# Q, K and V by one level of Strassen, with left-hand sums shared by the three products and with five-bank product chains

## The chip, the cores and the metric

The kernel runs on one core of a Trainium2 chip. The metric is the device time of one execution in microseconds (us). "Work of TensorE" below means matmuls counted in the trace, times the spacing that a steady stream of them shows in the same trace: 0.216 us for one with 512 columns, 0.06 us for one with 132. What a stage takes beyond its work is called "lost".

## The reference

```python
# x: 2048 x 1024, H = 32 heads of 32, F = 3584, all bf16
q, k, v = split(layernorm(x) @ wqkv)             # 3 products 2048x1024x1024
phi = lambda t: where(t > 0, t + 1, exp(t)) + 1e-6
kv  = einsum("bhsd,bhse->bhde", phi(k), v)       # needs every token
z   = einsum("bhsd->bhd", phi(k))
o   = (phi(q) @ kv) / (phi(q) @ z + 1e-6)
h   = x + o @ wo
hn  = layernorm(h)
out = h + (relu(hn @ W_gate) * (hn @ W_up)) @ W_down
```

## The kernel before

TensorE goes through five stages: a start-up; K, V and the sums kv over all 16 token tiles; Q, attention and four early blocks of the MLP, woven into each other; 24 wide MLP blocks; the down projection. MLP and down projection are computed by one level of Strassen already (7 products of half size instead of 8). Q, K and V are plain.

```python
abpool = tile_pool(name="abpool", bufs=2, space=PSUM)    # vp, attn
pspool = tile_pool(name="ps", bufs=3, space=PSUM)        # tp, kp, qp
ndpool = tile_pool(name="ndpool", bufs=3, space=PSUM)    # nd, in the attention stage
...
def kproj(t):                                  # one tile of 128 tokens
    for j in range(2):
        ps = bank("kp")
        for kc in range(KC):                   # 8 matmuls of 128x512
            nc.tensor.matmul(ps[:], lhsT=xnT[:, kc, t * P:(t + 1) * P],
                             rhs=wkv_sb[:, kc, j * NW:(j + 1) * NW], ...)
        phi_from_psum(ps[:], pk[:, j * NW:(j + 1) * NW], NW)
...
AHEAD = 2
for t in range(AHEAD): ln_T(t)                 # LayerNorm and transpose
for g in range(ST // NT):                      # 4 groups of 4 tiles
    for t in group(g):
        if t + AHEAD < ST: ln_T(t + AHEAD)     # stands before the first kproj
        pks[t] = kproj(t)
    for t in group(g): vproj_kv(t, pks.pop(t))
for c in range(KC): q_proj(qblocks[0], c)
...
LAG = (0, 1, 2, 3)             # a tile: nd, oT, output projection, transpose of hn
STS = ST // NS                 # 8 tiles in a half of the tokens
QSTEPS = 3 * ST // NS // 2     # 12 steps with Q in them
for step in range(QSTEPS):
    attn_step(step)            # tile n runs its stage k in step n + LAG[k]
    for b, c in rest[...]: q_proj(b, c)
psctx.close()
early = [load_group(g) for g in range(NE // GP)]   # weights of the early MLP blocks
for n, step in enumerate(range(QSTEPS, ST + 3)):
    attn_step(step)
    for p in flow[...]: p()    # parts of the early MLP blocks
```

When the last tile of a half has gone through `hn_T`, four VectorE additions of 128x2048 build the Strassen sums of that half; the first MLP blocks need those of the first half. All DMA of the kernel is issued from one queue, that of SyncE.

Of the kernel before, what the change touches and what calls it, by code (L numbers as in the profile page):

```python
# [8 lines left out]
ALU = mybir.AluOpType  # L9
# [22 lines left out]
def block_kernel(ctx: ExitStack, tc: tile.TileContext, x, wqkv, wo, wg, wu, wd, out, H: int):  # L32
# [41 lines left out]

    abctx = ExitStack()
    abpool = abctx.enter_context(tc.tile_pool(name="abpool", bufs=2, space=PSUM, side="right"))
    psctx = ExitStack()
    pspool = psctx.enter_context(tc.tile_pool(name="ps", bufs=3, space=PSUM))

    def bank(nm, dt=FP32, shape=None):  # L80
        return pspool.tile(shape or [P, NW], dt, tag="b", name=nm)
# [4 lines left out]
    pqT = pq_pool.tile([P, KC, S], BF16, name="pqT")  # L86
    kvz = pq_pool.tile([P, KC, NDW], BF16, name="kvz")
    wo_sb = pq_pool.tile([P, KC, D], BF16, name="wo_sb")
# [4 lines left out]
    qwork = qctx.enter_context(tc.tile_pool(name="qwork", bufs=2, side="right"))  # L93
    wq_sb = qpool.tile([P, KC, D], BF16, name="wq_sb")
    xnT = qpool.tile([P, KC, S], BF16, name="xnT")
    wqkv_v = wqkv.rearrange("(kc p) n -> p kc n", p=P)

    def phi_from_psum(ps_ap, dst_ap, width):
        e = qwork.tile([P, width], FP32, tag="phi_e", name="phi_e")
        nc.scalar.activation(out=e[:], in_=ps_ap, func=ACT.Exp)  # L100
        e2 = qwork.tile([P, width], FP32, tag="phi_e2", name="phi_e2")
        nc.vector.tensor_scalar(out=e2[:], in0=e[:], scalar1=1.0, scalar2=PHI_EPS,
                                op0=ALU.min, op1=ALU.add)
        nc.vector.scalar_tensor_tensor(out=dst_ap, in0=ps_ap, scalar=0.0, in1=e2[:],  # L104
                                       op0=ALU.max, op1=ALU.add)

    def q_proj(b, c):
        ps = bank("qp")
        for kc in range(KC):
            nc.tensor.matmul(ps[:], lhsT=wq_sb[:, kc, c * P:(c + 1) * P],  # L110
                             rhs=xnT[:, kc, b * SW:(b + 1) * SW], start=(kc == 0), stop=(kc == KC - 1))
        phi_from_psum(ps[:], pqT[:, c, b * SW:(b + 1) * SW], SW)

    def layernorm(src, stats, dst, small):

        mv = small.tile([P, nc.vector.BN_AGGR_DIM], FP32, tag="mv", name="mv")
        nc.vector.bn_aggr(out=mv[:], in_=stats[:])
        lnv = small.tile([P, 1], FP32, tag="lnv", name="lnv")
        nc.scalar.activation(out=lnv[:], in_=mv[:, 1:2], func=ACT.Ln, bias=LN_EPS, scale=1.0)
        rstd = small.tile([P, 1], FP32, tag="rstd", name="rstd")  # L120
        nc.scalar.activation(out=rstd[:], in_=lnv[:], func=ACT.Exp, scale=-0.5)
        nc.vector.tensor_scalar(out=dst[:], in0=src[:], scalar1=mv[:, 0:1], scalar2=rstd[:],
                                op0=ALU.subtract, op1=ALU.mult)
# [3 lines left out]
    qblocks = [order[k] // NT for k in range(0, ST, NT)]  # L127
# [3 lines left out]
    n_kv = (KC + GPB - 1) // GPB  # L131
    with ExitStack() as actx:
        apool = actx.enter_context(tc.tile_pool(name="apool", bufs=1))
        xpool = actx.enter_context(tc.tile_pool(name="xpool", bufs=6))
        awork = actx.enter_context(tc.tile_pool(name="awork", bufs=2))
        asmall = actx.enter_context(tc.tile_pool(name="asmall", bufs=4))
        wkv_sb = apool.tile([P, KC, 2 * D], BF16, name="wkv_sb")
        kvpool = actx.enter_context(tc.tile_pool(name="kvpool", bufs=n_kv, space=PSUM))
# [3 lines left out]
        def load_x(t):  # L142
            x_sb = xpool.tile([P, D], BF16, tag="x_sb", name="x_sb")
            nc.sync.dma_start(out=x_sb[:], in_=xf[t * P:(t + 1) * P, :])
            x_tiles[t] = x_sb
# [4 lines left out]
        load_x(0)  # L150
        load_w(wkv_sb, 0, D)
        load_x(1)
        load_w(wkv_sb, 1, D)
        load_x(2)
        load_x(3)
        load_w(wkv_sb, 2, D)
        load_w(wkv_sb, 3, D)
        load_x(4)
        load_x(5)
        for j in range(2):  # L160
            load_w(wq_sb, j, 0)
        nc.sync.dma_start(out=wo_sb[:], in_=wo.rearrange("(kc p) n -> p kc n", p=P))

        def ln_T(t):
            if t not in x_tiles:
                load_x(t)
            x_sb = x_tiles.pop(t)
            stats = asmall.tile([P, 2, nc.vector.BN_STATS_DIM], FP32, tag="stats", name="stats")
            for i in range(2):
                nc.vector.bn_stats(out=stats[:, i, :], in_=x_sb[:, i * NW:(i + 1) * NW])  # L170
            xn = awork.tile([P, D], BF16, tag="xn", name="xn")
            layernorm(x_sb, stats, xn, asmall)
            if t >= PE_T:
                nc.sync.dma_start_transpose(out=xnT[:, :, t * P:(t + 1) * P], in_=xn[:])
                return
            for i in range(2):
                pt = bank("tp", BF16, [P, KH, P])
                for kc in range(KH):
                    nc.tensor.transpose(pt[:, kc, :], xn[:, (i * KH + kc) * P:(i * KH + kc + 1) * P], ident[:])
                (nc.scalar.copy if i else nc.vector.tensor_copy)(  # L180
                    out=xnT[:, i * KH:(i + 1) * KH, t * P:(t + 1) * P], in_=pt[:])

        def kproj(t):
            pk = awork.tile([P, D], BF16, tag="pk", bufs=NT + 2, name="pk")
            for j in range(2):
                ps = bank("kp")
                for kc in range(KC):
                    nc.tensor.matmul(ps[:], lhsT=xnT[:, kc, t * P:(t + 1) * P],  # L188
                                     rhs=wkv_sb[:, kc, j * NW:(j + 1) * NW],
                                     start=(kc == 0), stop=(kc == KC - 1))  # L190
                phi_from_psum(ps[:], pk[:, j * NW:(j + 1) * NW], NW)
            return pk

        def vproj_kv(t, pk):
            v_sb = awork.tile([P, KC, NDW], BF16, tag="v_sb", name="v_sb")
            nc.gpsimd.memset(v_sb[:, :, P:NDW], 1.0)
            for j in range(2):
                ps = abpool.tile([P, NW], FP32, tag="ab", name="vp")
                for kc in range(KC):
                    nc.tensor.matmul(ps[:], lhsT=xnT[:, kc, t * P:(t + 1) * P],  # L200
                                     rhs=wkv_sb[:, kc, D + j * NW:D + (j + 1) * NW],
                                     start=(kc == 0), stop=(kc == KC - 1))
                nc.scalar.copy(out=v_sb[:, j * KH:(j + 1) * KH, 0:P],  # L203
                               in_=ps[:].rearrange("p (c e) -> p c e", e=P))
            for c in range(KC):
                bnk, i = divmod(c, GPB)
                nc.tensor.matmul(kv_ps[bnk][:, i * NDW:(i + 1) * NDW],
                                 lhsT=pk[:, c * P:(c + 1) * P], rhs=v_sb[:, c, :],
                                 start=(t == 0 and i == 0), stop=(t == ST - 1),
                                 skip_group_check=True)  # L210

        PE_T = 4
        AHEAD = 2
        for t in range(AHEAD):
            ln_T(t)
        for g in range(ST // NT):
            pks = {}
            for t in range(g * NT, (g + 1) * NT):
                if t + AHEAD < ST:
                    ln_T(t + AHEAD)  # L220
                pks[t] = kproj(t)
            for t in range(g * NT, (g + 1) * NT):
                vproj_kv(t, pks.pop(t))
# [4 lines left out]
        for c in range(KC):  # L228
            q_proj(qblocks[0], c)
# [3 lines left out]
    ndpool = psctx.enter_context(tc.tile_pool(name="ndpool", bufs=3, space=PSUM))  # L233
    aops = mctx.enter_context(tc.tile_pool(name="aops", bufs=1))

    hnT = [[aops.tile([P, KC, SW], BF16, name=f"hn{s}{i}") for i in range(2)] for s in range(NS)]
    hns = [[aops.tile([P, KH, SW], FP16, name=f"hs{s}{k}") for k in range(3)] for s in range(NS)]
    pieces = [(c, min(GPB, KC - c)) for c in range(0, KC, GPB)]

    def strassen_sums(out, a11, a12, a21, a22, eng):  # L240

        s1, s2, s3, s4 = out
        eng.tensor_tensor(out=s1, in0=a21, in1=a22, op=ALU.add)
        eng.tensor_tensor(out=s2, in0=s1, in1=a11, op=ALU.subtract)
        eng.tensor_tensor(out=s3, in0=a11, in1=a21, op=ALU.subtract)
        eng.tensor_tensor(out=s4, in0=a12, in1=s2, op=ALU.subtract)

    def hn_blocks(s):
        return [[hnT[s][i][:, j * KH:(j + 1) * KH, :] for j in range(2)] for i in range(2)]

    def attn_stages(t, late):
# [5 lines left out]
        def nd():  # L257
# [3 lines left out]
            for c0, n in pieces:  # L261
                ps = (abpool if late else ndpool).tile([P, NW], FP32, tag="ab" if late else "nd", name="nd")
# [12 lines left out]
        def oT():  # L275
            st["oT"] = bwork.tile([P, KC, P], BF16, tag="oT", name="oT")
            nc.sync.dma_start_transpose(out=st["oT"][:], in_=st["o"][:])
            x_sb = bwork.tile([P, D], BF16, tag="x_res", bufs=3, name="x_res")
# [372 lines left out]
```

## Time and profile before

788.15 us median of the first three runs (788.11 to 789.91). The head of the profile's page gives the span and each engine's busy time:

```profile
span 786.4 us, 9532 instructions
...
PE 755.9 (96%) x3602; PEld 347.9 (44%) x3664; DVE 459.1 (58%) x848; ACT 261.5 (33%) x457; POOL 3.6 (0%) x32
```

TensorE (PE) is 96% busy: it bounds the kernel. How its time falls into stages is read from its timeline (where the first matmul of each kind starts); the table of windows then gives the busy time of every engine in them. The rows are K/V, Q with attention and early MLP, the wide MLP blocks, and the down projection; the columns are length, busy time (with the number of instructions) of each engine, granted clock, DMA share and GB/s.

```profile
core 0: us, PE busy (x) PEld busy (x) DVE busy (x) ACT busy (x) POOL busy (x), PEclk, DMA share, GB/s
15.16:141.21 126.05, 123.03 (x640) 58.64 (x652) 57.54 (x118) 42.33 (x90) 2.00 (x14) 1.00 0.37 95
141.21:312.47 171.26, 165.51 (x835) 77.41 (x847) 124.71 (x347) 86.95 (x184) 0.00 (x0) 0.99 0.57 130
312.47:612.97 300.50, 295.40 (x1336) 132.83 (x1360) 169.83 (x280) 127.70 (x172) 0.00 (x0) 1.00 0.24 70
612.97:786.40 173.43, 169.06 (x775) 76.61 (x784) 98.98 (x89) 0.58 (x1) 0.00 (x0) 1.00 0.51 171
```

The first two rows hold the stages that the change touches.

```profile
312.47 1.03 PE L386 MATMUL A<-hn_1499,wg 128*128 128x512 bf16 x3
316.13 1.02 PE L386 MATMUL E<-hs_1503,wg 128*128 128x512 f16 x4 [0.29 <-DVE gu L405]
```

There is little waiting to remove. What can be removed is matmuls, and the start: TensorE's timeline (start, length, engine, line, operation, count, in brackets the idle time before it and what ended it) shows three tiles' transposes ahead of the first K matmul.

```profile
6.26 1.04 PE L179 MATMUL tp<-ident,xn 128*128 128x128 bf16 x8 [6.26 <-DVE xn L122]
10.22 1.04 PE L179 MATMUL tp<-ident,xn 128*128 128x128 bf16 x8 [2.92 <-DVE xn L122]
14.34 1.03 PE L179 MATMUL tp<-ident,xn 128*128 128x128 bf16 x8 [3.08 <-DVE xn L122]
15.16 5.09 PE L188 MATMUL kp<-wkv_sb,xnT 128*128 128x512 bf16 x13
```

The list of TensorE's waits (us in all, times, longest) has besides these only small entries:

```profile
PE tp L179 <- DVE xn L122: 12.3, 3, 6.3
PE nd L264 <- DVE o_sb L271: 2.2, 1, 2.2
PE A L386 <- ACT snap L400: 2.0, 2, 1.1
```

### The profile page before, as it was taken

The numbers are of one execution on the slowest core, as the hardware profiler recorded it, in microseconds if no ns is written. First come the engines' busy times: TensorE is split into PE (matmuls) and PEld (weight loads), VectorE is DVE, ScalarE is ACT, GpSimd is POOL, SyncE is SP. The second block draws the span as 40 slices with busy tenths as digits, with TensorE's granted clock in tenths as the row PEclk, the third lists the DMA queues.
The fourth block names the chain that finished last, engine by engine and source line by source line (L and its number), as shares of the span: only waits on it lengthen the run. The fifth ranks groups of instructions, "written<-read, shape, count | busy, mean of one in ns | idle before, by whom it ended". The sixth has DMA issues, their size and how long they took to land.

```text
span 786.4 us, 9532 instructions
## 1 busy us (share of the span) xinstructions
PE 755.9 (96%) x3602; PEld 347.9 (44%) x3664; DVE 459.1 (58%) x848; ACT 261.5 (33%) x457; POOL 3.6 (0%) x32
## 2 busy tenths in 40 slices
PE   3989999999998999999999999999999999999998
PEld 2444444444443444444444444444444444444443
DVE  4783412576688667757456464564644992439722
ACT  2333323346555545444434444444444000000000
POOL 0000000000000000000000000000000000000000
PEclk9999999999999999999999999999999999999999
DMA  9991000045659834453204032140100896881001
GB/s 319 308 188 27 1 1 1 1 93 133 151 111 263 194 101 120 155 140 92 64 33 128 8 99 55 35 127 8 46 5 31 271 285 206 299 307 50 27 28 53
DMA packets 125150, 89.76 MB, mean 114 GB/s; under 512 B 50352, under 2 KB 116912, under 8 KB 124592
## 3 DMA queue, kind: packets, MB, share of 16 engines
q1 hardware_dynamic: 125104, 89.15, 40.2%
q8 instruction: 28, 0.46, 0.3%
q14 instruction: 18, 0.15, 0.1%
HBM read 59.77 MB, written 17.83 MB: 99 GB/s over the span
## 4 chain that ended last, share of the span: by engine, by line
PE 63%; DVE 16%; ACT 6%; issue 4%; DMA 3%; SPq 0%; DVEq 0%; ACTq 0%
PE A L386 17%; PE accA L521 10%; PE E L386 9%; PE accE L521 6%; PE vp L200 5%; DVE gu L405 4%; PE kp L188 4%; PE qp L110 3%; PE Dp L386 3%; PE attn L288 3%; ACT snap L400 2%; PE accD L521 2%; ACT hn L300 1%; DVE x_res L290 1%; ACT gu L407 1%
## 5 line engine op out<-in xcount | busy, mean ns | idle before, releaser
L405 DVE TENSOR_TENSOR gu<-E,snap 128x1024 bf16<-128x1024 f32 x56 | 68.4, 1222 | 98.5 <-ACT snap L400 95.9
L400 ACT COPY snap<-A 128x1024 f32<-128x1024 f32 x84 | 84.0, 1007 | 92.3 <-PE A L386 92.2
L407 ACT ACTIVATE gu<-gu 128x512 bf16<-128x512 bf16 x84 | 52.9, 630 | 100.9 <-DVE gu L405 100.5
L521 PEld LDWEIGHTS <-hh 128*128 128x128 bf16 (+1 forms) x560 | 54.7, 98 | 67.7 <-issue 1.9
L521 PE MATMUL accA<-wd,hh 128*128 128x512 f16 (+1 forms) x333 | 73.2, 379 | 1.6 <-DVE gu L405 1.4
L386 PEld LDWEIGHTS <-tg 128*128 128x128 f16 x448 | 43.7, 98 | 59.3 <-issue 9.2
L386 PEld LDWEIGHTS <-tu 128*128 128x128 f16 x448 | 43.8, 98 | 52.6
L288 PE MATMUL attn<-wo_sb,oT 128*128 128x512 bf16 x250 | 60.0, 386 | 1.0 <-DVE rd L270 0.7
L188 PE MATMUL kp<-wkv_sb,xnT 128*128 128x512 bf16 x250 | 58.3, 389 | 1.2 <-DVE pk L104 0.8
L200 PE MATMUL vp<-wkv_sb,xnT 128*128 128x512 bf16 x249 | 59.2, 379 | 0.3
L110 PE MATMUL qp<-xnT,wq_sb 128*128 128x512 bf16 x250 | 57.0, 379 | 0.2
L386 PEld LDWEIGHTS <-wu 128*128 128x128 bf16 x336 | 32.9, 98 | 39.6
L386 PEld LDWEIGHTS <-wg 128*128 128x128 bf16 x336 | 32.7, 98 | 39.9 <-issue 1.6
L188 PEld LDWEIGHTS <-xnT 128*128 128x128 bf16 x256 | 25.3, 100 | 31.3 <-issue 4.1
L405 DVE TENSOR_TENSOR gu<-Dp,snap 128x1024 bf16<-128x1024 f32 x28 | 34.1, 1220 | 6.3 <-ACT snap L400 4.4
L110 PEld LDWEIGHTS <-wq_sb 128*128 128x128 bf16 x256 | 24.9, 98 | 29.0
L288 PEld LDWEIGHTS <-oT 128*128 128x128 bf16 x256 | 24.6, 99 | 29.0 <-issue 3.8
L200 PEld LDWEIGHTS <-xnT 128*128 128x128 bf16 x256 | 24.0, 98 | 24.3
L203 ACT CAST v_sb<-vp 128x512 bf16<-128x512 f32 x32 | 18.7, 584 | 39.0 <-PE vp L200 39.0
L386 PE MATMUL A<-hn_1500,tg 128*128 128x512 f16 (+1 forms) x111 | 28.7, 379 | 1.2 <-ACT snap L400 1.1
L300 ACT ACTIVATE hn<-x_res,sm 128x1024 bf16<-128x1024 bf16 x16 | 18.3, 1146 | 34.2 <-DVE sm L299 29.4
L386 PE MATMUL A<-hn_1498,tg 128*128 128x512 f16 (+1 forms) x112 | 28.7, 379 | 0.9 <-ACT snap L400 0.9
(359 smaller groups left out, 1016.2 us busy)
## 6 DMA issues: line engine op xcount, KB each, us to landing
wd<-in_B_W_down_dram SPq DMA_DIRECT2D x16, 896.0 KB, 6.5
wg<-in_B_W_gate_dram SPq DMA_DIRECT2D x14, 512.0 KB, 5.1
wu<-in_B_W_up_dram SPq DMA_DIRECT2D x14, 512.0 KB, 5.0
x_sb<-in_A_x_dram SPq DMA_DIRECT2D x16, 256.0 KB, 4.0
wkv_sb<-in_A_wqkv_dram SPq DMA_DIRECT2D x4, 1024.0 KB, 9.3
x_res<-in_A_x_dram SPq DMA_DIRECT2D x16, 256.0 KB, 3.1
out_dram<-o SPq DMA_DIRECT2D x32, 128.0 KB, 2.1
wq_sb<-in_A_wqkv_dram SPq DMA_DIRECT2D x2, 1024.0 KB, 11.0
```

Of the source, the lines that this page charges most:

```text
L110: nc.tensor.matmul(ps[:], lhsT=wq_sb[:, kc, c * P:(c + 1) * P], rhs=xnT[:, kc, b * SW:(b + 1) * SW], start=(kc == 0), stop=(kc == KC - 1))
L188: nc.tensor.matmul(ps[:], lhsT=xnT[:, kc, t * P:(t + 1) * P], rhs=wkv_sb[:, kc, j * NW:(j + 1) * NW], start=(kc == 0), stop=(kc == KC - 1))
L200: nc.tensor.matmul(ps[:], lhsT=xnT[:, kc, t * P:(t + 1) * P], rhs=wkv_sb[:, kc, D + j * NW:D + (j + 1) * NW], start=(kc == 0), stop=(kc == ...
L203: nc.scalar.copy(out=v_sb[:, j * KH:(j + 1) * KH, 0:P], in_=ps[:].rearrange("p (c e) -> p c e", e=P))
L288: nc.tensor.matmul(ps[:], lhsT=st["oT"][:, c, :], rhs=wo_sb[:, c, j * NW:(j + 1) * NW], start=(c == 0), stop=(c == KC - 1))
L290: nc.vector.scalar_tensor_tensor(out=h_sb[:, j * NW:(j + 1) * NW], in0=ps[:], scalar=1.0, in1=h_sb[:, j * NW:(j + 1) * NW], op0=ALU.mult, ...
L300: nc.scalar.activation(out=st["hn"][:], in_=h_sb[:], func=ACT.Square, bias=nmean, scale=1.0, accum_out=var)
L386: nc.tensor.matmul(ps[:, v, :], lhsT=w[v][m - 1][:, kc, :], rhs=left[m - 1][:, kc, :], start=(start and kc == 0), stop=(kc == KH - 1), ski ...
L400: nc.scalar.copy(out=m[:], in_=ps[:])
L405: nc.vector.tensor_tensor(out=gu[:], in0=ps[:], in1=m[:], op=ALU.add)
L407: nc.scalar.activation(out=gu[:, 0, :], in_=gu[:, 0, :], func=ACT.Relu)
L521: nc.tensor.matmul(accs[tt][:], lhsT=lhs[:, half * FD + f, tt * P:(tt + 1) * P], rhs=rhs[half][:, f, :], start=(start and half == 0 and f ...
```

## The change

It aims at TensorE's work. One Strassen unit covers four token tiles (K, V) or four 128-column strips of Q's output, with 56 matmuls instead of 64. K and V stay plain for the first four tiles, so that the kernel can start before any sums exist. Q's 256 matmuls become 224, the 512 of K and V become 464: 80 fewer, 17.3 us at 0.216 us each. The left-hand sums of the normalized x are made once and serve Q, K and V.

The products of a unit go through five PSUM banks (tags A and E with two each, D with one), and partial results are copied out by ScalarE ("snapshots"). The same chain, called `narrow`, now serves the four early MLP blocks. That leaves attention two `ab` banks and a single `nd` bank. Buffers are shared: K's weights lie where Q's result comes later, pk where `wo` comes later. The attention steps are arranged anew: Q's first half now comes before attention, its second half spreads over 10 steps (before, three quarters of Q over 12), and the second half of the tiles begins after the first has been started, with a gap of two steps (`begin_at`). The early MLP weights are loaded before attention begins.

```diff
-    abpool = ... tile_pool(name="abpool", bufs=2, space=PSUM)
-    pspool = ... tile_pool(name="ps", bufs=3, space=PSUM)
-    ndpool = ... tile_pool(name="ndpool", bufs=3, space=PSUM)
+    pspool = ... tile_pool(name="ps", bufs=1, space=PSUM)      # A 2, E 2, D 1
+    abpool = ... tile_pool(name="abpool", bufs=2, space=PSUM)
+    ndpool = ... tile_pool(name="ndpool", bufs=1, space=PSUM)
+    def strassen(pool, work, mm, fin, sbufs=3):
+        for v in range(2):
+            A[v] = pool.tile([P, NW], FP32, tag="A", bufs=2, name="Aq")
+            mm(A[v], 1, v, True); snap(v, "m1")
+        yield
+        m2(0)                                    # bank D
+        for v in range(2):
+            mm(A[v], 6, v, False); snap(v, "u2")
+        m2(1)
+        yield
+        ...                                      # E: 5; A: 7, snap u3; A: 4; E: 3
+        # K and V
+        ln_T(atiles[0]); ln_T(atiles[1])         # kp may go between the transposes
+        for t in units[0]: k_plain(t); ln_T(todo.pop(0))
+        ...
+        for u in range(1, NU):
+            for _ in k_unit(u): ...
+            for t in units[u - 1]: kv_tile(t)
+            for n, _ in enumerate(v_unit(u)): ...
+    # Q and attention
+    early = [load_group(g) for g in range(NE // GP)]
-    QSTEPS = 3 * ST // NS // 2
+    QSTEPS = STS + 2
+    begin_at = [n if n < STS else n - STS + QSTEPS for n in range(ST)]
...
+    for step in range(QSTEPS):
+        attn_step(step)
+        for p in rest[...]: next(p)              # Q units of the second half
+    for step in range(QSTEPS, STS + LAG[3]):
+        if step == QSTEPS: flow.pop(0)()         # first early MLP product
+        attn_step(step)
+    for n in range(steps): attn_step(...); ...   # the rest, with the early MLP blocks
```

## The prediction

> **What bounds the kernel now.** TensorE. The page gives PE 96% busy (755.9 of 786.4 us), DVE 58%, ACT 33%. In the chain of waits 56 down-projection matmuls take 12.09 us, 0.216 us each (the Trainium skill, "TensorE: Matmul & The Clock Gate", "Wait — 56ns, not 53.3ns?", states 215.7 ns warm and 426.7 ns cold; the first kp matmuls in the timeline are indeed 0.427 us apart). A 132-column matmul goes every 0.06 us. By the PE timeline: start-up until the first kp matmul at 15.2 us; K, V and kv until 141.2; Q, attention and four early MLP blocks until 312.5; 24 MLP blocks until 613; down projection until 783. Matmul counts times 0.216 give about 122, 167, 290 and 169 us for the last four, so the two stages that change hold only about 4 us each of TensorE waiting.
>
> **Removed.** K, V and Q were 768 matmuls of 512 columns. After: K and V keep the first four token tiles plain (128) and take 3 units of 56 each (336); Q takes 4 units of 56 (224). 688 in all; the instruction order confirms 80 matmuls fewer: 80 x 0.216 = 17.3 us, all on the engine that bounds. 10.4 us belong to K/V, 6.9 to Q.
>
> Also at the start: today three tiles' transposes stand before the first kp matmul, which waits for VectorE (12.3 us of "tp waits for xn"). The new order puts kp after the first tile's transposes, so it should begin near 11 us. Gain about 3 us, less a wait of VectorE for the second half of K's weights (its b12-b11 sum stands early in the queue).
>
> **Added.** VectorE: right-hand sums of three weights, 12 x 1.22 us = 15 us; left sums 16 x about 0.65 = 10 us; bf16 phi work about equal. LayerNorm's scaling (0.54 us each) leaves VectorE. ScalarE: snapshots and copies, 8 x 0.59 per unit, 47 us in all; LayerNorm's Identity 16 x 1.2 = 19 us. Both engines stay under TensorE in total, but VectorE is about as long as TensorE up to the first V unit (about 70 us), and near 85% in the Q/attention stage (today 74%).
>
> **New waits.** (a) Product 4 follows product 7 on the same bank with only one group (0.86 us) between, and the snapshot takes 0.59 us plus latency: any longer ScalarE instruction (1.2 us) in its way stalls TensorE. (b) One D bank. (c) nd pieces have one bank instead of three, with a den, rd, o_sb chain of at least 1.2 us (0.27 + 0.20 + 0.5 + hand-over) covered by 5 to 9 matmuls (1.1 to 1.9 us). 48 pieces. I guess 0.2 us each beyond today. (d) The change of PSUM pools before the MLP blocks, 1 to 2 us.
>
> **Sum.** K/V: -10.4, -3 start, +2 to 3 waits: ends near 130. Q/attention: -6.9, +6 waits: about 170 us, barely shorter. MLP blocks and down projection unchanged. 788 - 15 = 773 us, 80% range 766 to 784. Chance of faster by over 2%: 0.45; within 2%: 0.50; slower: 0.05.
>
> **What would show it.** PE busy falls to about 740; first kp at 10 to 12 us; TensorE reaches Q near 130 us, not 141; the next stage nearly as long as before, with waits "nd for o_sb" and "Aq for snap" of several us in the list of waits; VectorE above 80% there; MLP blocks still 300 us, down projection 170.
>
> **What would make it wrong.** If VectorE's queue lags more than I think in the first V unit or the nd chain stalls by 0.5 us a piece, the gain vanishes. If the scheduled order covers all waits, 767 us.

## The result, and the profile after

776.15 us median of four runs (773.99 to 777.15), beside 788.13 (787.84 to 789.91) for the kernel before. The ratio is 0.984, with a 95% interval from 0.9814 to 0.9866: within the 2% that count as the same. Here and below a ratio is the mean time of one kernel's fast runs over that of the other's of the same rounds, so it is not quite the ratio of the medians. Executions over 1.5% slower than the fastest of the same kernel are left out of the means. The profiled run took 775.71 us.

```profile
span 773.6 us, 9575 instructions
...
PE 742.8 (96%) x3584; PEld 337.9 (44%) x3584; DVE 490.0 (63%) x924; ACT 313.6 (41%) x529; POOL 3.5 (0%) x34
```

```profile
9.45:124.68 115.23, 111.90 (x619) 54.51 (x617) 85.89 (x164) 72.39 (x123) 1.62 (x11) 1.00 0.40 106
124.68:301.44 176.76, 167.24 (x835) 74.64 (x833) 131.82 (x385) 111.67 (x231) 0.00 (x0) 0.98 0.56 135
301.44:600.11 298.67, 293.11 (x1346) 131.32 (x1344) 169.66 (x280) 125.64 (x169) 0.00 (x0) 1.00 0.24 72
600.11:773.60 173.49, 169.53 (x784) 76.60 (x784) 99.06 (x89) 0.57 (x1) 0.00 (x0) 1.00 0.51 171
```

The four last rows are the same four stages as before. Reading both tables together:

| us | before | after | difference |
|---|---|---|---|
| until the first K matmul | 15.2 | 9.5 | -5.7 |
| K, V, kv | 126.0 | 115.2 | -10.8 |
| Q, attention, four early MLP blocks | 171.3 | 176.8 | +5.5 |
| 24 wide MLP blocks | 300.5 | 298.7 | -1.8 |
| down projection, to the end | 173.4 | 173.5 | +0.1 |

The third and fourth rows are not quite like for like. The 16 early matmuls (3.5 us) that the kernel before runs after the first wide matmul stand within the stage in the change (1344 weight loads in the third row, not 1360). Counted with their stage in both kernels, Q with attention and early MLP grew by 2.0 us, not 5.5, and the wide blocks by 1.6.

TensorE's busy time fell by 13.1 us only, although 17.3 us of matmul work are gone: the trace of before lacks 62 matmuls beside its weight loads, and some matmuls of the change ran at half clock. The change is 16.5 us ahead when TensorE reaches Q, and then, in the stage in which it has another 6.9 us of matmuls less, it falls back by 5.5 (2.0 like for like). That stage lost 17.0 us, where before it lost 8.5. (The texts before the runs say 17.5 and 4.6. The 4.6 takes all four early blocks to lie before 312.47 us; for the 17.5, 704 matmuls at 0.216 us and 128 at 0.06 give 17.0.) The start works as intended: transposes and K matmuls alternate.

```profile
7.12 0.61 PE L261 MATMUL tp<-ident,xn 128*128 128x128 bf16 x4 [7.12 <-ACT xn L254]
9.07 0.58 PE L261 MATMUL tp<-ident,xn 128*128 128x128 bf16 x4 [1.34 <-DVE xT L262]
9.45 1.48 PE L309 MATMUL kp<-pq_mem,xT 128*128 128x512 bf16 x3
11.19 0.58 PE L261 MATMUL tp<-ident,xn 128*128 128x128 bf16 x4 [0.26 <-ACT xT L262]
```

TensorE's waits, beside those of before:

```profile
PE tp L261 <- ACT xn L254: 7.1, 1, 7.1
PE attn L497 <- DMA oT<-o_sb: 5.8, 7, 2.5
PE Dq L609 <- DVE gu L618: 2.4, 2, 1.2
...
PE nd L473 <- DVE o_sb L480: 1.0, 1, 1.0
...
PE Aq L276 <- ACT u L143: 0.9, 1, 0.9
```

Two waits expected in the prediction, nd for o_sb (1.0 us) and Aq for the snapshots (0.9 and 0.7), are there and small. The largest new one is another: the output projection waits for oT, a DMA transpose of attention's result. The issues of SyncE's queue around the first of them (SPq, x2 means two issues in a row) show why:

```profile
153.47 1.00 SPq L453 DMA_DIRECT2D wg<-in_B_W_gate_dram  x2
154.53 2.81 SPq L453 DMA_DIRECT2D wu<-in_B_W_up_dram  x2
157.38 3.46 SPq L453 DMA_DIRECT2D wg<-in_B_W_gate_dram  x2
160.89 3.79 SPq L453 DMA_DIRECT2D wu<-in_B_W_up_dram  x2
164.80 5.34 SPq L486 DMA_TRANSPOSE oT<-o_sb  x2
```

The first tile's o_sb was complete at 155.6 us. Its transpose was issued at 164.80, behind eight weight loads, for MLP blocks that begin at 208.6. The first output projection starts at 171.3 us.

A second hole lies where one half of the tiles ends and the next has just begun. TensorE's timeline there:

```profile
211.11 3.63 PE L497 MATMUL attn<-wo_mem,oT 128*128 128x512 bf16 x16 [0.26 <-DMA oT<-o_sb]
...
216.72 0.81 PE L609 MATMUL Dq<-hn,wu 128*128 128x512 bf16 x3 [1.16 <-DVE gu L618]
...
219.06 0.59 PE L609 MATMUL Dq<-hn,wg 128*128 128x512 bf16 x2 [1.19 <-DVE gu L618]
...
221.27 0.51 PE L473 MATMUL nd<-kvz,pq_mem 128*128 128x132 bf16 x3 [1.02 <-DVE o_sb L480]
222.65 1.89 PE L497 MATMUL attn<-wo_mem,oT 128*128 128x512 bf16 x4 [0.87 <-DMA oT<-o_sb]
...
226.69 1.60 PE L609 MATMUL Eq<-hs,tg 128*128 128x512 f16 x4
```

The last output projection of the first half runs from 211.1 to 214.6 us. What needs its result (residual sum, LayerNorm, transpose, sums of hn, then Eq<-hs) comes at 226.7. In between stand only the few MLP products that need no sums, and the first nd pieces of the next half. The windows, cut to 3.4 us, show what follows from it:

```profile
214.20:217.60 3.40, 2.24 (x15) 1.11 (x14) 3.25 (x11) 1.84 (x5) 0.00 (x0) 1.00 0.52 96
217.60:221.00 3.40, 1.46 (x9) 0.46 (x6) 3.39 (x12) 2.12 (x6) 0.00 (x0) 1.00 0.50 164
221.00:224.40 3.40, 2.26 (x8) 0.89 (x9) 1.38 (x4) 0.27 (x1) 0.00 (x0) 0.50 0.84 177
224.40:227.80 3.40, 3.40 (x11) 1.36 (x10) 3.40 (x5) 0.27 (x1) 0.00 (x0) 0.50 0.18 69
227.80:231.20 3.40, 3.40 (x18) 1.53 (x17) 1.92 (x4) 1.17 (x2) 0.00 (x0) 1.00 0.76 43
```

The third column from the end is the granted clock. TensorE was busy for 1.46 of 3.40 us, and for the next 6.8 us it was granted half its clock. Before has a half-clock stretch of 3.4 us in this stage. Three of the four runs of the change have a mean clock of 0.996 and took 775.7 to 777.2 us; the fourth, at 1.0, took 773.99: 1.7 to 3.2 us less. That fits a half clock that is a part of the loss, and not the larger one.

### The profile page after: what moved, and what is told of

Read it like the earlier page. It is cut to its first block, busy times and chain, and to the rows that moved or that the text cites. A ratio compares the mean times of both kernels' runs of the same rounds, so it can differ in the third digit from the quotient of the medians.

```text
span 773.6 us, 9575 instructions
## 1 busy us (share of the span) xinstructions
PE 742.8 (96%) x3584; PEld 337.9 (44%) x3584; DVE 490.0 (63%) x924; ACT 313.6 (41%) x529; POOL 3.5 (0%) x34
## 4 chain that ended last, share of the span: by engine, by line
PE 44%; DVE 11%; ACT 3%; issue 2%; DMA 1%; DVEq 0%
PE A L576 15%; PE accA L737 10%; PE E L576 8%; PE accE L737 6%; DVE gu L595 4%; PE Dp L576 3%; ACT snap L590 2%; PE accD L737 2%; DVE hh L598 1%; DMA out_dram<-o 1%; ACT gu L597 1%; DVE hh L651 1%; DVE tg L559 1%; DVE tu L556 1%; DVE tg L556 1%
## 5 line engine op out<-in xcount | busy, mean ns | idle before, releaser
L497 PE MATMUL attn<-wo_mem,oT 128*128 128x512 bf16 x256 | 62.9, 388 | 5.8 <-DMA oT<-o_sb 5.8
L598 DVE TENSOR_TENSOR hh<-gu 128x512 bf16<-128x512 bf16 x72 | 30.4, 423 | 38.1 <-ACT gu L597 38.1
L576 PE MATMUL A<-hn,tg 128*128 128x512 f16 (+1 forms) x192 | 49.3, 379 | 1.1 <-ACT snap L590 1.1
L576 PE MATMUL A<-hn,tu 128*128 128x512 f16 (+1 forms) x192 | 49.3, 379 | 0.0
L143 ACT COPY u<-Aq 128x512 f32<-128x512 f32 x56 | 32.0, 581 | 29.2 <-PE Aq L276 19.1
L737 PEld LDWEIGHTS <-s 128*128 128x128 f16 x224 | 21.9, 98 | 27.2 <-issue 0.8
L276 PEld LDWEIGHTS <-xT 128*128 128x128 bf16 (+1 forms) x192 | 18.6, 98 | 24.8 <-issue 3.1
L480 DVE TENSOR_TENSOR o_sb<-nd,rd 128x384 bf16<-128x384 f32 (+1 forms) x48 | 24.5, 510 | 4.3 <-DMA oT<-o_sb 2.1
L499 DVE SCALAR_TENSOR_TENSOR x_res<-attn,x_res 128x512 bf16<-128x512 f32 x32 | 21.9, 684 | 7.0 <-PE attn L497 6.6
L576 PE MATMUL A<-hs,tg 128*128 128x512 f16 x96 | 24.6, 379 | 1.1 <-ACT snap L590 1.1
```

Of the source, the lines that this page charges most:

```text
L143: nc.scalar.copy(out=snaps[nm, v], in_=A[v][:])
L276: nc.tensor.matmul(ps[:], lhsT=left[m - 1][:, kc, r + v * P:r + (v + 1) * P], rhs=right[m - 1][:, kc, :], start=(start and kc == 0), stop= ...
L480: nc.vector.tensor_tensor(out=ov[:, c0:c0 + n], in0=ndv[:, :, 0:P].rearrange("p k (h e) -> p k h e", h=HPC), in1=rd[:, 0:n, :].unsqueeze(3 ...
L497: nc.tensor.matmul(ps[:], lhsT=st["oT"][:, c, :], rhs=wo_sb[:, c, j * NW:(j + 1) * NW], start=(c == 0), stop=(c == KC - 1))
L499: nc.vector.scalar_tensor_tensor(out=h_sb[:, j * NW:(j + 1) * NW], in0=ps[:], scalar=1.0, in1=h_sb[:, j * NW:(j + 1) * NW], op0=ALU.mult, ...
L576: nc.tensor.matmul(ps[:, v, :], lhsT=w[v][m - 1][:, kc, :], rhs=left[m - 1][:, kc, :], start=(start and kc == 0), stop=(kc == KH - 1), ski ...
```

## The experiments

The theory after reading the traces: (1) the matmuls taken out of K/V and Q are worth what they should be; (2) what is given back comes from how the Q and attention stage is arranged. There were three candidates: the loads ahead of oT in the queue, the single nd bank, and the two steps without a new tile. The rival: Strassen itself (snapshots, phi, sums on VectorE and ScalarE) slows the stage. Another rival was not tried: no run puts the four early MLP blocks back on the chain that they had before.

### The loads later: load_late

```diff
-    early = [load_group(g) for g in range(NE // GP)]
+    early = []
     for step in range(QSTEPS):
         attn_step(step)
+        if step in (4, 6):
+            early.append(load_group(len(early)))
```

> The changed kernel with one move: the two groups of early gate and up weights are issued in attention steps 4 and 6 of the second stage, not before its first step. Stage 2 is from the first Q matmul to the first wide MLP matmul: 171.3 us before, 176.8 us in the changed kernel. Queue theory: in the changed kernel the first oT transpose was issued at 164.8 us although its o_sb was ready at 155.6, because eight weight loads stand ahead of it in the DMA queue; freed of them, the waits of attn for oT (5.8 us) nearly vanish, the bubble before the first MLP sums shrinks too, stage 2 falls to 166 to 171 us and the total to 766 to 771 us. Bank theory (one nd bank, one D bank) and VectorE theory (the added snapshots and phi work): the queue only happened to be first, stage 2 stays within 2 us of 176.8, total 774 to 777.

Measured: 776.44 us (774.87 to 777.63), ratio 0.9848 [0.9829, 0.9866]; nothing gained against the change. In the trace the loads still begin at 152.9 us, but the transposes now go between them. The first output projection moved from 171.3 to 159.4 us, and the waits for oT fell from 5.8 to 3.2 us. But the first wide MLP block began at 300.6 us instead of 301.4, because a new wait took the place of the old one. From its list of TensorE's waits:

```profile
PE Eq L611 <- DVE hs L111: 4.6, 1, 4.6
PE attn L496 <- DMA oT<-o_sb: 3.2, 4, 2.0
```

The queue is the cause of the oT waits, as the 12 us show, but not of the lost time: work done earlier piles up before the same hole.

### Three shared banks for nd and attn: nd3

```diff
-    abpool = ... bufs=2
-    ndpool = ... bufs=1
+    abpool = ... bufs=3
-                ps = ndpool.tile([P, NW], FP32, tag="nd", name="nd")
+                ps = abpool.tile([P, NW], FP32, tag="ab", name="nd")
```

> The changed kernel, but nd and the output projection share three PSUM banks, instead of one bank for nd and two for the projection. Bank theory: nd pieces no longer wait for the one bank, stage 2 (176.8 us) falls by 4 us or more, total 772 or less. Queue theory: the first attn matmul still waits for its oT transpose until about 171 us, stage 2 changes by less than 2 us, total 774 to 778.

Measured: 775.0 us (774.04 to 778.43), ratio 0.9845 [0.9818, 0.9872]. The wait for oT is still 4.9 us, that of nd for o_sb is 2.2 us (1.0 with the one bank). Alone the bank isn't the cause either.

### K and V plain: kv_plain

```diff
-            for _ in k_unit(u):
+            for t in units[u]:
+                k_plain(t)
...
-            for n, _ in enumerate(v_unit(u)):
+            for t in units[u]:
+                v_plain(t)
```

The sums of x are still made, after K and V, for Q.

> The changed kernel with K and V of all token tiles plain (64 matmuls per unit of four tiles, not 56), Q still by Strassen; start-up and buffers as in the changed kernel. The first Q matmul is at 141.2 us before and 124.7 us in the changed kernel, 16.5 us earlier. Matmul account: 48 matmuls x 0.216 = 10.4 us of it are Strassen's, about 6 us the start-up's (first kp at 9.5 us, not 15.2): first Q matmul at 133 to 136 us here, less about 3 us of waits in the first units if Strassen had caused them; total 783 to 787 us. Start-up account: the waits in the first Strassen units eat most of the saving, first Q matmul below 129 us, total below 780 us.

Measured: 787.37 us (785.37 to 788.71), ratio 0.9985 [0.9967, 1.0004]. TensorE reaches Q at 134.6 us: 9.9 us later than with the change, where 48 matmuls are worth 10.4, and 6.6 earlier than before, 5.0 of it because the first K matmul stands at 10.1 us and not at 15.2. Strassen in K and V earns what its matmuls are worth, and the early start is a gain of its own. The total lies just above the range expected from the matmul account (783 to 787). The stage after it is again long: 178.5 us from the first Q matmul to the first wide block. So K/V Strassen isn't what slows that stage.

### Q plain: q_plain

```diff
-        left = left_ops(xT[s], xS[s])
-        ...                                     # 7 half products per unit
+                        for kc in range(KC):    # 8 matmuls, in the banks A and E
+                            nc.tensor.matmul(ps[:], lhsT=wq_sb[:, kc, ...], rhs=xT[s][i][:, kc, :], ...)
+                        ...                     # phi as in the kernel before
```

The block of x that had been overwritten by a sum is restored by a subtraction.

> The changed kernel with Q plain (256 matmuls, not 224; the block that the sums of normalized x had overwritten is restored by a subtraction), K and V by Strassen. Matmul account: 32 matmuls x 0.216 = 6.9 us more, total 781 to 784 us. VectorE theory: Strassen's snapshots and its longer phi in Q are what lengthened stage 2 (176.8 us, though it holds 6.9 us less matmul work), so plain Q costs nothing or gains: stage 2 at most 177 us, total 776 or less. Queue theory: the late oT transposes stay, but TensorE has 6.9 us more Q work to fill the waits with, so the total moves by less than 4 us either way.

Measured: 781.8 us (781.62 to 783.4), ratio 0.9921 [0.9906, 0.9936]: 5.7 us slower than the change by the medians, where the 32 matmuls are worth 6.9. The stage took 182.0 us with 166.7 us of work and lost 15.3 us, nearly as much as with Strassen (17.0). The rival falls as far as Q goes: its snapshots and sums cost at most 1 to 2 us of the stage's loss (the change's profile also has 3.4 us more of half clock in it). What the early MLP blocks' new chain costs is not shown by it.

### The change once more: after_again

No edit.

> The changed kernel itself, as a yardstick on this chip: 774 to 777 us, stage 2 about 177 us with about 17 us in which no matmul starts in time.

Measured: three fast runs, 775.55 to 778.02 us, ratio 0.9843 [0.9819, 0.9867], which confirms the first result. A fourth run took 1318.91 us with a granted clock of 0.56.

### Both, and the steps spread wider: late_nd3, late_spread, late_nd3_spread

late_nd3 is load_late and nd3 together. The "spread" kernels have Q over 12 steps as before, so that fewer Q products fall into each. The same number sets where the second half of the tiles begins, so the gap between the halves grows from two steps to four:

```diff
-    QSTEPS = STS + 2
+    QSTEPS = STS + 4
...
-    ready = STS + LAG[3]
+    ready = max(QSTEPS, STS + LAG[3])
```

> Both single moves together: early weight loads issued in attention steps 4 and 6, and three PSUM banks shared by nd and the output projection. Each alone left 16 to 17 us of lost time in stage 2 (changed kernel 17.5). Stacked-limits theory: each was hidden behind the next; together they leave less than 13 us, stage 2 at most 172 us, total 771 or less. Coupling theory (the first half's last token tiles and the whole of the second half's Q must end before anything new is ready, so a hole at the change to the MLP blocks remains however the work before it is arranged): the hole of 5 us or more moves but stays, total 773 to 777.

> Early weight loads in attention steps 4 and 6, and the twelve pieces of the second half's Q handed out over twelve attention steps, not ten, so that more of Q is left for the hole before the first MLP sums. Stacked-limits theory: with one nd bank left in place, at most 2 us of gain: total 773 to 777. Coupling theory: only Q work that is left when the last output projection of the first half ends can fill the hole; the instruction order leaves 17 matmuls (3.7 us) there, about as in the run with the late loads alone, so also little gain.

> All three together: late weight loads, three banks for nd and projection, Q pieces over twelve steps. In the instruction order the projections now come in whole groups of 16 with nd and Q between them, and 24 Q matmuls (5.2 us) follow the last projection of the first half. Stacked-limits theory: stage 2 at most 170 us, lost time below 11 us, total at most 769 us. Coupling theory: the hole before the first MLP sums shrinks by no more than the 5.2 us of Q left in it; total 771 to 775.

Measured: late_nd3 772.35 us (771.77 to 775.87), ratio 0.98 [0.9773, 0.9826]; late_spread 776.32 (774.85 to 779.15), 0.9845 [0.9818, 0.9872]; late_nd3_spread 772.43 (770.12 to 774.68), 0.9801 [0.9777, 0.9825]. The theory of stacked limits had 771 us or less for late_nd3 and 769 or less for late_nd3_spread: missed by 1.4 and 3.4. Late loads and three banks, each worth nothing by itself, are worth some 4 us together (the interval just overlaps that of after_again, of the same rounds). Once nothing waits for oT (late_nd3's list has no such wait any more), the pieces need the banks; without the late loads the banks have nothing to do earlier: that is my reading, no run tests it. A wider spread with a wider gap adds nothing; the two are not told apart.

### No gap between the halves: no_gap

One number is changed, so that the second half of the tiles begins in the step after the first half's last. It also puts the second half of Q into 8 steps instead of 10:

```diff
-    QSTEPS = STS + 2
+    QSTEPS = STS
```

> The changed kernel with one number altered: the second half's attention begins right after the first half's (8 attention steps that hand out Q, not 10), so its tiles overlap the last steps of the first half. Coupling theory: the hole before the first MLP sums (about 8 us of the 17.5 us lost in stage 2) is there because the changed kernel leaves two empty steps between the halves; with tiles 8 to 10 in it the loss falls by 4 us or more, total 772 or less. Stacked-limits theory: with one nd bank and the weight loads first in the queue the other waits stay or grow, less than 3 us of gain, total 773 to 777.

Measured: 771.81 us (770.2 to 773.44), ratio 0.9791 [0.9769, 0.9813]. The change has 0.984 [0.9814, 0.9866] to the same kernel before, so this is half a per cent or some 4 us faster than the change. The stage is 172.0 us instead of 176.8 (four early matmuls, 0.9 us, lie after it here), with no half-clock stretch in it, though the waits for oT have stayed. From its list of TensorE's waits:

```profile
PE attn L497 <- DMA oT<-o_sb: 5.7, 8, 2.3
```

Its window of 3.4 us at the place of the hole:

```profile
217.60:221.00 3.40, 3.40 (x19) 1.56 (x20) 2.92 (x12) 1.90 (x6) 0.00 (x0) 1.00 1.01 205
```

In the window in which the change had 1.46 us of TensorE work this one has 3.40, all of it nd pieces and output projections; no Q matmul stands there. So what fills the hole is attention that the gap had put off. In the change as it is, the gap between the halves costs 4 to 5 us together with the half clock that it brings.

### All three: no_gap_late_nd3, and with split sums: no_gap_late_nd3_split

The first has the edits of load_late, nd3 and no_gap. The second also makes the sums of hn in two parts of 256 columns, the first of them two tiles earlier:

```diff
-                if k == 3 and (n + 1) % STS == 0:
-                    left_sums(hnT[...], hns[...], slice(0, SW))
+                if k == 3 and n % STS in (STS - 3, STS - 1):
+                    h = (n % STS) // 2 - 2
+                    left_sums(hnT[...], hns[...], slice(h * 2 * P, (h + 1) * 2 * P))
```

> No gap between the halves, with late weight loads and three banks for nd and projection. Without the first of these, the other two gave 772.4 us (stage 2 172.9 us, 13.7 lost). Both theories together: the hole goes as well, lost time in stage 2 at most 8 us as in the kernel before (4.6), stage 2 at most 168 us, total 765 to 769. If the loss comes from VectorE and ScalarE work that Strassen's Q added, and not from the arrangement, the waits only move: stage 2 170 us or more, total 771 or more.

> The same, with the left sums of the normalized residual made in two halves of 256 columns, the first after six tiles, as the changed kernel does for x. The last tile then waits for VectorE ops of about 0.65 us in place of 1.22 us. If the hole still waits for the sums: 1 to 2 us less than without the split. If the attention of the second half fills the hole by itself: within 1 us of it. Total 764 to 769.

Measured: 771.07 us (769.24 to 771.97, five runs), ratio 0.9774 [0.9754, 0.9794]; split 770.77 (770.03 to 771.52), 0.9778 [0.976, 0.9795]. The parts don't add: beside no_gap (0.9791) the other two edits, worth 4 us without it, are worth about 1 us, within the intervals. The split is worth nothing. The stage of no_gap_late_nd3 is still 171.7 us and lost 12.9. That misses what both theories together had led to expect (765 to 769 us, 8 us lost) and lies in the range that stood for work added on VectorE and ScalarE. Nor does the gap's length count for much once the other two edits are in: with no step, two and four the ratios are 0.9774, 0.98 and 0.9801, with intervals that overlap. Where the hole was, VectorE now looks nearly full (the third pair of columns, 25.62 of 28 us, in the split kernel):

```profile
200.00:228.00 28.00, 22.03 (x121) 10.41 (x120) 25.62 (x83) 16.29 (x38) 0.00 (x0) 1.00 0.62 150
```

That suggested a new limit, the amount of VectorE's work, and it was put to the test.

### Ten us of VectorE's work taken away: one_sums

In no_gap_late_nd3 the right-hand sums of the first early MLP block serve all four. The result is wrong. (The comparison with the reference doesn't see these four blocks, and so says nothing about them.)

```diff
-            st["q"] = quad_steps(0, f, sums(early[f // GP], f % GP), None)()
+            if f == 0:
+                one.append(sums(early[0], 0))
+            st["q"] = quad_steps(0, f, one[0], None)()
```

> The kernel of no_gap_late_nd3 (771.07 us, stage from the first Q matmul to the first wide MLP block 171.8 us, of which 13.4 us lost by TensorE), with three of the four early MLP blocks using the right-hand sums of the first block: 24 VectorE instructions of 0.42 us, 10 us in all, leave VectorE between 200 and 300 us; TensorE's work is unchanged. The result is wrong on purpose. Theory A (what is left of the loss is the amount of VectorE's work in the stretch where it was 83 to 91% busy): stage 2 shrinks by 3 to 6 us and the time falls to 765 to 768 us. Rival B (what is left are hand-overs, chains of short instructions between three engines, which are as long with fewer sums in the queue): stage 2 within 1.5 us of 171.8, time 769.5 to 772. Between the two, 768 to 769.5 us, would say that both count.

Measured: 769.45 us (768.49 to 770.2, five runs), ratio 0.976 [0.9745, 0.9776], beside 0.9774 [0.9754, 0.9794] with the sums: about 1 us, with intervals that overlap. By the letter that lies in the band in which both count, 0.05 us from the rival's range and 1.45 from theory A's. All its runs had a clock of 1.0. The two runs of no_gap_late_nd3 at 1.0 took 769.24 and 769.59 us, no longer than these; its three at 0.998 took 771.07 to 771.97, so that even the 1 us may be the half clock alone. The profiled run, the fastest of the five, has the stage at 169.7 us, 2.0 less than no_gap_late_nd3's profile with its 3.4 us of half clock. The windows show where the 10 us leave from:

```profile
200.00:228.00 28.00, 22.83 (x117) 10.29 (x116) 23.30 (x77) 15.93 (x38) 0.00 (x0) 0.94 0.64 153
228.00:302.00 74.00, 71.08 (x349) 32.49 (x348) 54.27 (x142) 42.08 (x85) 0.00 (x0) 1.00 0.50 127
```

```profile
200.00:228.00 28.00, 22.66 (x121) 10.56 (x122) 24.63 (x75) 16.75 (x38) 0.00 (x0) 1.00 0.68 151
228.00:302.00 74.00, 71.19 (x345) 32.77 (x351) 47.86 (x124) 42.26 (x86) 0.00 (x0) 1.00 0.49 130
```

The first fence is no_gap_late_nd3, the second one_sums. From 200 to 228 us VectorE is no less busy than it was (24.63 us, 23.30 with the sums), and TensorE is busy no longer (22.66 and 22.83; it took in six more weight loads in that time, at full clock throughout). Most of what was taken away, 6.4 of the 10 us, lay after that stretch. So the run shows that 10 us of VectorE's work are worth about 1 us, perhaps nothing: the total of that work is not the limit of the stage. It doesn't test the 28 us by themselves. TensorE's remaining waits are nearly the same in both kernels, and short: in no_gap_late_nd3, from 165 us on,

```profile
PE attn L495 <- DVE o_sb L478: 3.0, 6, 0.7
PE Dq L610 <- DVE gu L619: 1.4, 1, 1.4
PE Eq L610 <- DVE gu L619: 1.3, 1, 1.3
```

## Why the prediction was right or wrong

The time was predicted as 773 us, range 766 to 784, and "within 2%" had the highest chance. 776.15 lies in the range and in that class. Inside the sum two terms were mis-sized in opposite directions, by some 6 us each, and they nearly cancelled: that the total came so close is in part luck. (The terms as written add up to about -12 us, 776; the 15 that was taken off is not their sum.)

- **"Removed: 17.3 us", right.** K/V fell by 10.8 us against 10.4 predicted. kv_plain gave 9.9 back, and q_plain 5.7 of Q's 6.9.
- **"Gain about 3 us" at the start, too small.** The first K matmul stands at 9.45 us, not at 10 to 12; the gain is 5.7 us. One tile's transposes stand before it, as predicted, and they end sooner than I worked out; no run tests why.
- **"Plus 2 to 3 us of waits" in K/V, wrong.** The stage lost 5.9 us after and about 7 before. The feared wait for the snapshot before product 4 comes to 0.9 and 0.7 us in all. TensorE reached Q at 124.7 us, not near 130.
- **"Q/attention: -6.9, +6 waits: about 170", the step that failed.** The stage took 176.8 us. Of the 6 us or so beyond the prediction, 3.5 are early MLP matmuls that the prediction's boundary at 312.5 us had left with the wide blocks; the new lost time is 8.5 us (17.0 - 8.5), 2.5 above the guess. The size of the waits was thus not far off, but the causes named for them were wrong: nd for o_sb costs 1.0 us and not 0.2 us for each of 48 pieces, the snapshots less than 2, and three banks alone gained nothing (nd3). I costed each instruction and each bank, and didn't lay the steps of the weave side by side: the loads ahead of the transposes in one queue, and the two steps in which no tile begins. no_gap shows the second at 4 to 5 us, in the change as it is. The first shows its worth only together with the banks (late_nd3, 4 us).
- **"VectorE above 80% there", too high:** 131.82 of 176.76 us, 75%. The extra work on VectorE and ScalarE in Q did little (q_plain lost 15.3 us, the change 17.0), and one_sums shows that VectorE's total isn't the limit even in the best version.
- **"MLP blocks and down projection unchanged", nearly:** -1.8 and +0.1 us by the table, +1.6 and +0.1 with the 16 early matmuls counted elsewhere. The change of PSUM pools, predicted at 1 to 2 us, is in it with 2.1 (two waits of 1.10 and 1.00 us).
- **"PE busy falls to about 740", right:** 742.8 us.

Still open is what the 12.9 us of loss in this stage consist of in no_gap_late_nd3, 4.4 us more than in the kernel before. Some 3 us are output projections that wait for o_sb, some 3 are MLP products that wait for gu, each below 1.5 us, and a half-clock stretch of 3.4 us comes in some runs. Neither more banks, nor earlier loads, nor split sums, nor less VectorE work removed them. The early MLP blocks' new chain, with its single bank D, was not taken out in any run and may have a part in it. My view that they are hand-overs between three engines in short chains is argued, not shown.

## What to carry to other kernels

Taking matmuls out of a TensorE-bound kernel need not pay their full price where a stage has other steps woven into it: here the straight K/V stage became 10.8 us shorter for 10.4 us of matmuls, while the woven stage lost 8.5 us more than before and so took back more than its own 6.9. Count the work on both sides of a stage's boundary before you compare two kernels by it; here 16 matmuls lay on the other side. Before you build, lay the steps of the weave side by side, and look for steps where nothing new begins and for loads that stand in the transposes' queue. The Trainium skill ("Perfetto Trace Analysis", "Optimization Strategy") advises interleaving regimes with different limits and following each gap to what ends it. On the gaps this case agrees (the hole followed that way is worth 4 to 5 us in no_gap; no run here tests the interleaving itself), with the addition that a fix may be worth nothing alone and 4 us with a second one (load_late, nd3, late_nd3), so try them in pairs before you drop them. The best version is no_gap_late_nd3: three small edits to the change, 771.07 us, ratio 0.9774 to before. That it beats no_gap with its one number (0.9791) is not shown: the intervals overlap.

## What the Trainium skill lacked or had wrong

- "TensorE: Matmul & The Clock Gate", "Back-to-back issue gap", gives about 131 ns for a 512-column matmul in a sustained stream of weight loads and matmuls. Here a stream with one weight load for each matmul runs at 0.216 us (56 of the down projection in 12.09 us), which is the page's own figure for the isolated gap.
- The same page, "HAM oscillation — how this bites in real kernels", puts the rule for a warm clock as no idle gap above about 3.4 us. Here the change's clock was halved after a window whose longest gap was 1.19 us. In these traces each half-clock stretch inside a kernel lasts 3.41 us or twice that. Cut into windows of that length, counted from the changes of the clock, the traces of the 13 fast runs show this: each window at full clock with at most 1.45 us of TensorE busy time was followed by half clock, none with 1.53 us or more was, and of those between (1.46 to 1.51) some were and some were not. That points to the share of busy time in a window; the page speaks of many small idle times too, but names no share.
- The same page tells of the clock "stuck" at a quarter for 50 us and more. It names no lasting state of a single busy core like that of after_again's first run: a granted clock of 0.555, with three stretches of 0.5, from 14.5 us to the end, which took 1318.91 us.
- "DMA: Bandwidth & Descriptors", "Issuing engines are not separate DMA queues", calls the time to initiate a DMA usually small beside the DMA. Here the first two loads of 512 KB took 0.5 us each to issue, where one takes 5 to 6 us to land; but the eight held the issuing queue from 153.47 to 164.7 us, up to 1.9 us each, and a transpose that was ready at 155.6 waited behind them. The share of the DMA engines was 1.03 in that time, so the queue may have been held by the transfers and not by the issuing; no run separates the two.
